# The third quarter of the first weights, loaded behind batch 0's gathers, and a new order of all steps

## The chip, the cores and the metric

The kernel runs on one core of a Trainium2 chip. Five engines work side by side and each takes its own queue strictly in program order: PE (TensorE, matrix products; PEld is its weight load), DVE (VectorE), ACT (ScalarE), POOL (GpSimd) and SP (SyncE, which here only issues DMAs). The metric is the time of one execution on the device in microseconds (us).

## The reference

Eight batches of eight heads, 576 positions, 64 values per head. Attention is masked (four heads see the last 32 positions, four see every 32nd), its output is laid side by side to rows of 512, a two-dimensional Fourier transform is added, and each row goes through a normalised two-layer network.

```python
def _attn_ref(q, k, v):
    scores = scale * np.matmul(q, k.transpose(0, 1, 3, 2))
    ...
    scores = np.where(masks[None, :, :, :], scores, -1000000000.0)
    ...
    return np.matmul(attn, v).astype(np.float32)

def _moe_ref(x, w_ch1, w_ch2):
    X = np.fft.fft(x, axis=1)
    X = np.fft.fft(X, axis=2)
    mixed = np.real(X).astype(np.float32)
    u = x + mixed
    mu = np.mean(u, axis=-1, keepdims=True)
    var = np.mean((u - mu) ** 2, axis=-1, keepdims=True)
    un = (u - mu) / np.sqrt(var + 1e-06)
    ch = np.maximum(un @ w_ch1, 0.0) @ w_ch2
    return (u + ch).astype(np.float32)
```

Here w_ch1 is 512 x 2048 and w_ch2 is 2048 x 512. Both arrive as 64-bit floats.

## The kernel before

**Stages.** Each batch goes through attention for four pairs of heads (`att_first` for batch 0, `att_pair32` and `att_pair` for the others), whose outputs `xo` are written to a buffer `xd` in DRAM. From there `fft_load` reads the first half of the rows in order (`xa`, line 820, on SP) and the mirrored rows by four gathers on POOL (line 824, into the third part of `xa` and the three of `xb`). `fft_batch` folds the rows on DVE and POOL (E and O are sum and difference of `xa` and `xb`, then `tmp` and `FD`, all line 834), and two products follow: A (lines 977 and 978 for batch 0, 931 and 932 later) against tables of cosines and sines and B (1003; 954 later). Their sum with x is `u`, the input of the network. `u` is cut into 18 chunks of 256 rows. Each chunk is normalised, transposed by DMA (`uT`, line 1084), multiplied with the first weights in eight steps (`ups`, line 1278, into `ph`) and with the second weights in eight (`downs`, line 1317, into `acc`). These two lines hold most of PE's work, and all products are made with 16-bit halves, three products for one.

**The weights.** Each of the two weight matrices comes in 16 pieces of 128 x 512, 64 bits an element. `weights` loads one into a staging buffer (line 1104 where there is a fixed place, 1108 from a pool) and turns the 64-bit patterns into 32-bit floats by hand: two passes on ACT (1113 and 1117; the second also on DVE, 1119), one on DVE (1123), then the sign, another on DVE (1129) or on ACT and POOL. `gram_piece` multiplies each piece with itself on PE (1158). After each four pieces of the first weights, `quarter` takes the norms from that product (1176 to 1178, a small product at line 332, `scales`), and `split` makes the two 16-bit halves with the scale so found (1197 on ACT, 1199 on DVE). `weights2` does the same for all 16 pieces of the second weights at once, and `scaled` splits them (1232, 1234), with a DMA (1236) to put one half in its place. The first `downs` needs these. While a gram is open, `rest` fills PE's planned pauses with products of a zero matrix (line 1166), whose results change nothing.

**Where the third quarter stands.** Pieces 0 to 7 of the first weights are loaded into the place of their own later results. Pieces 8 to 11 are loaded into the tiles that held q and k of batch 0 (`q0s`, by `stg1`), so a load has to wait until that head's scores are made. Pieces 12 to 15 are taken into buffers of later phases, behind the event `xb0`, which batch 0's gathers set.

**What sets the order.** There is no hand-written order. Every step is a generator that yields an `Op` with an engine, a planned duration, buffers that it takes (`get`) and returns (`put`), events it needs and sets. `Order.run` is a small simulator inside the kernel's construction: it takes the step that can start first on its engine, and among those that can start within a small window (the `W..` numbers) the one of lowest bias. What it picks is emitted to the engine's queue, so the plan fixes the order of every queue, and the chip then runs each queue in order as semaphores allow. The biases, windows, lead times and penalties are the numbers of `P`: for example `c` for the tables of batch 0 (`consts`), `w0a` for pieces 0 to 11, `w0` for 12 to 15, `GL` the time allowed to land for the gathers of batches 1 to 7, `GL0` for batch 0's. `vo` says behind which head's q and k the value tables are loaded, and `S0` and `S1` in which staging buffers pieces 12 to 15 and those of the second weights land.

The plan is made in two parts. In the first part are `att_first`, pieces 0 to 11 with quarters 0 to 2, `consts`, and `fft_batch(0)` up to product A, which needs the event `second`. It is run until nothing more can go; then the buffers of the start are given up and `second` is set. So in every queue all steps of the first part come before all of the second. In `consts` and for pieces 12 to 15 a helper `late` ties the first DMA that is issued after the gathers to the last gather, by a real wait; all behind it on SP's queue wait with it.

Of the kernel before, what the change touches and what calls it, by code (L numbers as in the profile page):

```python
# [19 lines left out]
B, H, S, D = 8, 8, 576, 64  # L20

P = dict(
    SL2=1.57, SLD2=2.778, GL0=8, LAT=0.637, GL=6.45, t2=9.759, l0=-28.888, a0=-20, sq0=7.465, w0a=25.925, c=-26.309,
    z=12.736, f0=-22.976, w0=-25.887, s0=-1.061, w1=2.262, s1=-12.582, p0=-14.949, p1=10.996, pn=-3.093, a1=-18.418,
    f1=-1.718, a2=1.463, f2=8.266, an=8.66, fn=-33.229, db=1.762, up=20.1, dn=20.114, ev=0.829, WS=0.0, WV=0.068,
    WA=0.0, WG=0.789, WT=0.095, SL=0.0, SLD=1.95, np=3, AL=3.136, SG=2.918, Lcl=0.553, Lfs=-0.174, Lwl=4.986,
    Lul=-7.793, LO=-11.521, LE=4.84, Lc2=-1.49, LSD=-13.798, Lsub=2.836, Lsub0=20.543, Lrt=20.361, Lu=4.381,
    ORD0=(3, 2, 0, 1), vo=([], [], [], [0, 1, 2, 3]), S0=('qk', 'qk', 'kt', 'pt'),
    S1=('kt', 'pt', 'f6', 'u', 'uT', 'qk', 'f6', 'kt', 'uT', 'u', 'f6', 'kt', 'pt', 'uT', 'u', 'f6'), HB=4, RB=1,
)  # L30
ORD0 = P["ORD0"]
FP32 = {(b, hp) for b in range(3) for hp in range(4)}
# [121 lines left out]
AL, SG = P["AL"], P["SG"]  # L154
# [19 lines left out]
WT = {e: P["W" + e] for e in "SVAGT"}  # L174
# [95 lines left out]
op = Op  # L270
# [3 lines left out]
def body(ctx: ExitStack, tc: tile.TileContext, a, out):  # L274
# [14 lines left out]
    SL, SLD = P["SL"], P["SLD"]  # L289
# [88 lines left out]
    def att_pair(b, hp):  # L378
# [20 lines left out]
        A.activation(jk[0:vp, 0:vw], vn[0:vp, 0:vw], AF.Square, accum_out=ss[0:vp, 2:3])  # L399
        yield op("T", 0.06, get="big", note=f"total {nm}", slack=P["SL2"])  # L400
        pn = psbig(f"n{nm}")[:, 0:3]
# [43 lines left out]

        yield op("T", 0.75 if local else 0.6, get="big", put="kt", note=f"scores {nm}", slack=P["SL2"])
        ps = psbig(f"s{nm}")
# [172 lines left out]
    def att_first(sp, pw):  # L620
# [11 lines left out]
        G.memset(pbt, 0.0)  # L632
        f6s = {hp: f6(f"pt0_{hp}") for hp in ORD0}
        for hp in ORD0:
# [195 lines left out]
    def fft_batch(b, xab=None):  # L830
# [85 lines left out]
        for gs in ((0, 1), (2,), (3, 4)):  # L916
            first, last = gs[0] == 0, gs[-1] == 4
            endT = yield op("T", 0.5 * len(gs), get="big f6 -fft" if first else "acc" if one and len(gs) == 1 else "big", need=f"FH{257 if last else 0}_{b} csin second", put="f6" if last else "", note=f"A{gs[0]} {b}", slack=P["SL2"] if b > 2 else SL if b else 0)
            if first:
# [28 lines left out]
        for t in range(3):  # L948
            r = 128 if t < 2 else 33
            yield op("T", 0.68, get=("acc" if one else "big") + (" u" if t < 2 else ""), need=" ".join(f"AT{g}_{b}" for g in (0, 2, 3)) + " dftd", put="f6" if t == 2 else "", at=endT, note=f"B{t} {b}", slack=P["SL2"] if b > 2 else SL if b else 0)  # L950
            ps = psone(b, f"B{b}_{t}")[:, 0:512]
# [144 lines left out]
    def weights(wi, i):  # L1096


        src, W, _ = list(wpieces(wi))[i]
        kind = STG[wi][i]  # L1100
        if kind is None:
            yield op("S", 1.45, need=f"sc{ORD0[(i - 8) // 2]}" if i >= 8 else "", note=f"ld {wi} {i}")
            stg = stg1(i)
            nc.sync.dma_start(stg, src)
        else:
            yield op("S", 1.45, get=kind, need="xb0", note=f"ld {wi} {i}")
            stg = stg2(kind, f"sa{wi}_{i}")
            late(nc.sync.dma_start(stg, src))
        wds = stg.bitcast(I32).rearrange("p (n t) -> p n t", t=2)
        wl, wh = wds[:, :, 0], wds[:, :, 1]  # L1110
        yield op("A", 0.67, note=f"c1 {wi} {i}")

        A.activation(wh.bitcast(F32), wh.bitcast(F32), AF.Copy, scale=2.0**-112)
        o = op("A", 0.67, note=f"cl {wi} {i}", alt=dict(V=(0.47, P["Lcl"])))
        yield o
        if o.engine == "A":
            A.activation(wl, wl.bitcast(U32), AF.Copy, scale=2.0**-29 * (1 - 2.0**-10), bias=-0.499)
        else:
            V.tensor_scalar(wl, wl, 29, None, op0=ALU.logical_shift_right)
        yield op("V", 0.8, need=f"w0_{i}" if wi else "", note=f"c2 {wi} {i}")  # L1120
        F = W.rearrange("p a b -> p (a b)").bitcast(F32)
        Fi = F.bitcast(I32)
        V.scalar_tensor_tensor(out=Fi, in0=wh, scalar=3, in1=wl, op0=ALU.logical_shift_left, op1=ALU.bitwise_or)  # L1123
        spawn(gram_piece(wi, i, F))

        o = op("V", 0.8, note=f"c3 {wi} {i}", alt=dict(A=(0.67, SG)))
        yield o
        if o.engine == "V":
            V.scalar_tensor_tensor(out=Fi, in0=wh, scalar=-(2**31), in1=Fi, op0=ALU.bitwise_and, op1=ALU.bitwise_or)  # L1129
        else:  # L1130
            A.activation(wl.bitcast(F32), wh.bitcast(F32), AF.Sign)
            yield op("G", 1.4, note=f"c4 {wi} {i}")
            G.tensor_tensor(out=F, in0=F, in1=wl.bitcast(F32), op=ALU.mult)
        yield op(o.engine.replace("A", "G"), 0, put=kind or "", sets=f"sign{wi}_{i}", note=f"c5 {wi} {i}")
# [314 lines left out]
```

## Time and profile before

| | |
|---|---|
| time, median of 3 runs | 983.55 us (978.34 to 986.63) |
| the profiled execution: time | 983.61 us |
| its span, first to last instruction | 981.8 us |
| PE busy | 939.3 us, 96% |
| DVE busy | 574.7 us, 59% |
| ACT busy | 452.2 us, 46% |
| POOL busy | 286.3 us, 29% |
| fill products (line 1166), all before 120 us | 427, 34.0 us of PE's busy time |
| granted PE clock, mean | 0.973 |

Busy time counts the fill products and the half-speed stretches too, so 96% isn't all useful work. A span of 40 equal slices is 24.5 us each in the page; the row of the granted clock there is 7, 8, 6, 8, 9, 9, 8 tenths in the first seven and 9 in all later ones. Nearly all that isn't steady lies in the first 200 us. In the rows below, "idle before" in brackets is the time that the engine waited ahead of the instruction, and behind the arrow stands what ended that wait by the profile; x is a count of instructions merged into one row, and a row can have short pauses in it.

### The profile page before, as it was taken

To read this page: it belongs to the slowest core of one execution; us is meant where nothing else is said; L and a number is where in the kernel's file an instruction comes from. 1 tells how busy PE (TensorE), PEld (TensorE's weight loads), DVE (VectorE), ACT (ScalarE), POOL (GpSimd) and SP (SyncE) were. 2 spreads that over 40 slices of the span, in tenths; PEclk is the share of its full clock that TensorE was granted. 3 is DMA by queue.
4 is the path that set the end of the run, shared out by engine and by line. 5 is a ranking of instruction groups with operands and counts; after the bars stand their busy time and mean duration, and the time that the engine had idled before them with its cause. 6 is when DMAs were issued, how large, how long until landed. Compare 5 with 4: busy or idle time off the path is not lost.

```text
span 981.8 us, 23873 instructions
## 1 busy us (share of the span) xinstructions
PE 939.3 (96%) x10017; PEld 659.7 (67%) x10018; DVE 574.7 (59%) x1129; ACT 452.2 (46%) x891; POOL 286.3 (29%) x297
## 2 busy tenths in 40 slices
PE   6779879999999999999999999999999999999998
PEld 6657764676766667676766676667666676676674
DVE  5785896756888588758765957587727221202000
ACT  2744765354565366555745564556423322222121
POOL 0120221223433343334324422442334122222121
PEclk7868998999999999999999999999999999999999
DMA  9757536804533644184537442743240101201000
GB/s 296 240 196 262 170 109 213 187 17 134 133 104 83 150 154 113 35 173 136 123 70 191 97 113 39 225 96 97 59 120 11 34 18 33 32 12 43 1 23 21
DMA packets 135452, 107.12 MB, mean 109 GB/s; under 512 B 103337, under 2 KB 113833, under 8 KB 135345
## 3 DMA queue, kind: packets, MB, share of 16 engines
q1 hardware_dynamic: 132784, 97.22, 37.0%
q0 software_dynamic: 2560, 8.39, 2.8%
q8 instruction: 78, 1.28, 0.6%
q14 instruction: 30, 0.24, 0.1%
HBM read 64.24 MB, written 18.89 MB: 85 GB/s over the span
## 4 chain that ended last, share of the span: by engine, by line
PE 82%; DVE 8%; DMA 5%; ACT 2%; issue 1%; SPq 1%; POOL 0%; ACTq 0%; DVEq 0%; POOLq 0%
PE ph L1278 35%; PE acc L1317 35%; PE B L954 2%; DMA uT<-unp 2%; PE A L931 1%; PE s L456 1%; DMA W<-in_w 1%; DVE W L1123 1%; PE o L487 1%; PE A L978 1%; PE A L977 1%; DMA mloc<-in_mloc 1%; DVE W L1129 1%; PE o L494 1%; DMA q<-in_w 1%
## 5 line engine op out<-in xcount | busy, mean ns | idle before, releaser
L1278 PE MATMUL ph<-uT,W 128*128 128x256 f16 x3456 | 395.4, 273 | 3.3 <-DMA uT<-unp 2.1
L1317 PE MATMUL acc<-W,h 128*128 128x512 f16 x1728 | 390.1, 381 | 2.1 <-POOL ss L393 1.6
L1278 PEld LDWEIGHTS <-W 128*128 128x128 f16 x3456 | 335.2, 98 | 53.8 <-DMA uT<-unp 2.4
L1296 POOL TENSOR_TENSOR h<-hf,h 128x512 f16<-128x512 f32 x144 | 184.5, 1282 | 461.2 <-ACT h L1294 337.8
L1317 PEld LDWEIGHTS <-h 128*128 128x128 f16 x1728 | 166.5, 98 | 191.7 <-issue 5.8
L1293 ACT ACTIVATE hf<-ph 128x512 f32<-128x512 f32 x144 | 85.8, 596 | 299.3 <-PE ph L1278 268.1
L1294 ACT ACTIVATE h<-ph 128x512 f16<-128x512 f32 x144 | 85.3, 592 | 0.0
L1325 DVE SCALAR_TENSOR_TENSOR u<-acc,cout,u 128x512 f32<-128x512 f32 x32 | 23.3, 745 | 101.5 <-PE acc L1317 100.4
L1082 DVE TENSOR_TENSOR unp<-un,unp 128x512 f16<-128x512 f32 x36 | 33.5, 932 | 48.3 <-ACT unp L1079 48.2
L1073 DVE TENSOR_SCALAR un<-u,mv,rstd 128x512 f32<-128x512 f32 x32 | 19.1, 596 | 52.1 <-POOL rstd L1066 50.8
L1066 POOL TENSOR_TENSOR rstd<-mv,negh 128x1 f32<-128x1 f32 x36 | 23.5, 657 | 76.1 <-DVE mv L1063 75.9
L433 DVE SCALAR_TENSOR_TENSOR kt<-qk,sc,kt 128x576 f16<-128x576 f32 (+1 forms) x40 | 36.6, 954 | 12.0 <-ACT kt L418 9.0
L1045 ACT ACTIVATE pq<-B,fcm 128x128 f32<-128x128 f32 (+7 forms) x105 | 27.3, 377 | 16.0 <-PE B L954 8.2
L1166 PE MATMUL gram<-oneb,zero 128*128 128x128 bf16 x427 | 34.0, 246 | 0.0
L468 ACT ACTIVATE sm<-sm 128x594 f32<-128x594 f32 (+1 forms) x20 | 16.3, 816 | 34.8 <-DVE sm L751 34.7
L1166 PEld LDWEIGHTS <-zero 128*128 128x128 bf16 x427 | 30.9, 113 | 2.0 <-issue 1.2
L418 ACT ACTIVATE kt<-qk,sc 128x576 f16<-128x576 f32 (+1 forms) x40 | 29.4, 788 | 3.9 <-DVE sc L374 3.2
L1079 ACT CAST unp<-un 128x512 f16<-128x512 f32 x36 | 22.1, 615 | 16.9 <-DMA uT<-unp 8.8
L1037 DVE TENSOR_TENSOR rt<-pq 128x257 f32<-128x257 f32 (+1 forms) x42 | 17.1, 449 | 21.7 <-ACT pq L1045 19.4
L751 DVE TENSOR_TENSOR sm<-sm,mx 128x594 f32<-128x594 f32 (+1 forms) x32 | 29.4, 919 | 0.3
L749 DVE TENSOR_REDUCE mx<-sm 128x11 f32<-128x594 f32 (+1 forms) x32 | 29.0, 907 | 0.4
L944 DVE SCALAR_TENSOR_TENSOR AT<-A,AT 128x290 f16<-128x290 f32 (+3 forms) x35 | 15.4, 481 | 21.5 <-ACT AT L939 20.5
(202 smaller groups left out, 1044.8 us busy)
## 6 DMA issues: line engine op xcount, KB each, us to landing
qk<-in_qk SPq DMA_DIRECT2D x28, 592.0 KB
sa<-in_w SPq DMA_DIRECT2D x20, 512.0 KB
out<-u SPq DMA_DIRECT2D x32, 256.0 KB
vn<-in_vl SPq DMA_DIRECT2D x10, 432.0 KB
W<-in_w SPq DMA_DIRECT2D x8, 512.0 KB
xd<-xo SPq DMA_DIRECT2D x16, 256.0 KB
xa<-xd SPq DMA_DIRECT2D x8, 512.0 KB
vn<-in_vs SPq DMA_DIRECT2D x10, 384.0 KB
```

Of the source, the lines that this page charges most:

```text
L418: A.activation(hi, src, AF.Copy, scale=f)
L433: V.scalar_tensor_tensor(out=lo, in0=src, scalar=f, in1=hi, op0=ALU.mult, op1=ALU.subtract)
L749: V.tensor_reduce(out=mx[:, 0:nb], in_=sm, axis=AX.X, op=ALU.max)
L751: on(o).tensor_tensor(out=sm, in0=sm, in1=mx[:, 0:nb].rearrange("p (g o) -> p g o", o=1).to_broadcast([128, nb, w]), op=ALU.subtract)
L1045: A.activation(dst, ps[0:r, c0:c1], AF.Copy, scale=cm[0:r])
L1082: on(o).tensor_tensor(out=unp[:, 1], in0=un, in1=unp[:, 0], op=ALU.subtract)
L1166: T.matmul(idle[-1][:, 0:128], zerb, oneb, start=False, stop=False)
L1278: T.matmul(ph[:, i, :], W1[:, 4 * (f0 // 512) + d, x, f0 % 512 : f0 % 512 + 128], self.uhl[y][:, d, :], start=(n == 0), stop=(n == 11))
L1293: A.activation(hf, ph, AF.Relu, scale=HS)
L1294: A.activation(hh, ph, AF.Relu, scale=HS)
L1296: G.tensor_tensor(out=hl, in0=hf, in1=hh, op=ALU.subtract)
L1317: T.matmul(self.acc[s], (hh, hl)[x][:, i, 128 * s : 128 * s + 128], W2[:, f, 1 - y, :], start=(f == 0 and n == 0), stop=(f == 15 and n == 2))
```

## The change

One line of `weights` changes: what the loads of pieces 8 to 11 need in the plan. Before it was the event that the scores of the head are made whose tile the piece takes; now it is `xb0`, that batch 0's gathers have landed. The staging place stays the same. Beside it, most of the numbers of `P` change, and with them the order of all queues; among them `vo`, so that the value tables of batch 0 are loaded between the heads' q and k instead of behind all of them, and `S1`, the staging places of the second weights.

```diff
 P = dict(
-    SL2=1.57, SLD2=2.778, GL0=8, LAT=0.637, GL=6.45, t2=9.759, l0=-28.888, a0=-20, sq0=7.465, w0a=25.925, c=-26.309,
-    z=12.736, f0=-22.976, w0=-25.887, s0=-1.061, w1=2.262, s1=-12.582, p0=-14.949, p1=10.996, pn=-3.093, a1=-18.418,
-    f1=-1.718, a2=1.463, f2=8.266, an=8.66, fn=-33.229, db=1.762, up=20.1, dn=20.114, ev=0.829, WS=0.0, WV=0.068,
-    WA=0.0, WG=0.789, WT=0.095, SL=0.0, SLD=1.95, np=3, AL=3.136, SG=2.918, Lcl=0.553, Lfs=-0.174, Lwl=4.986,
-    Lul=-7.793, LO=-11.521, LE=4.84, Lc2=-1.49, LSD=-13.798, Lsub=2.836, Lsub0=20.543, Lrt=20.361, Lu=4.381,
-    ORD0=(3, 2, 0, 1), vo=([], [], [], [0, 1, 2, 3]), S0=('qk', 'qk', 'kt', 'pt'),
-    S1=('kt', 'pt', 'f6', 'u', 'uT', 'qk', 'f6', 'kt', 'uT', 'u', 'f6', 'kt', 'pt', 'uT', 'u', 'f6'), HB=4, RB=1,
+    SL2=0.915, SLD2=2.5, GL0=8, LAT=0.97, GL=20.106, t2=9.759, l0=-30.073, a0=-19.177, sq0=7.465, w0a=20.686,
+    c=-24.962, z=2.714, f0=-26.63, w0=-28.483, s0=0.533, w1=1.247, s1=-14.997, p0=-16.817, p1=10.038, pn=-3.534,
+    a1=-17.166, f1=-1.58, a2=10.531, f2=1.591, an=11.643, fn=-36.503, db=1.762, up=20.1, dn=20.117, ev=0.829, WS=0.0,
+    WV=0.071, WA=0.0, WG=0.677, WT=0.154, SL=0.0, SLD=1.664, np=3, AL=3.818, SG=2.188, Lcl=2.011, Lfs=-0.174,
+    Lwl=4.927, Lul=-1.506, LO=-10.812, LE=4.723, Lc2=-1.124, LSD=-15.782, Lsub=8.559, Lsub0=20.543, Lrt=20.361,
+    Lu=4.381, ORD0=(3, 2, 0, 1), vo=([], [0], [1, 2], [3]), S0=('qk', 'qk', 'kt', 'pt'),
+    S1=('u', 'pt', 'f6', 'kt', 'qk', 'uT', 'f6', 'kt', 'uT', 'u', 'f6', 'kt', 'pt', 'uT', 'u', 'f6'), HB=4, RB=1,
 )
 ...
         if kind is None:
-            yield op("S", 1.45, need=f"sc{ORD0[(i - 8) // 2]}" if i >= 8 else "", note=f"ld {wi} {i}")
+            yield op("S", 1.45, need="xb0" if i >= 8 else "", note=f"ld {wi} {i}")
             stg = stg1(i)
             nc.sync.dma_start(stg, src)
```

Nothing is computed otherwise: the same products, the same loads, in another order.

## The prediction

> **What bounds the kernel now.** I read the page's head first, then a table of busy time by stage, then the queues around the moved loads one by one.
>
> ```profile
> span 981.8 us, 23873 instructions
> PE 939.3 (96%) x10017; PEld 659.7 (67%) x10018; DVE 574.7 (59%) x1129; ACT 452.2 (46%) x891; POOL 286.3 (29%) x297
> ```
>
> ```profile
> 40.00:64.80 24.80, 15.54 (x196) 13.69 (x194) 22.89 (x40) 10.35 (x20) 9.37 (x9) 0.81 0.83 313
> 64.80:79.80 15.00, 14.66 (x42) 8.47 (x43) 5.67 (x13) 7.33 (x13) 1.09 (x1) 0.50 0.31 107
> 79.80:107.40 27.60, 23.29 (x347) 19.92 (x348) 23.30 (x53) 18.27 (x33) 1.13 (x2) 0.95 0.83 266
> 107.40:148.90 41.50, 31.62 (x437) 27.61 (x435) 34.38 (x67) 25.60 (x44) 14.18 (x9) 0.98 0.42 128
> ...
> 200.00:981.80 781.80, 775.16 (x8001) 533.49 (x7999) 425.23 (x840) 349.13 (x710) 246.31 (x260) 1.00 0.34 84
> ```
>
> In the second fence the columns are stage and length, then busy time of PE, PEld, DVE, ACT and POOL, then the granted clock, the DMA share and GB/s. From 200 us to the end PE is busy 775.16 of 781.8 us at clock 1.00. No reordering can shorten that stretch by more than its 6.6 us of idle time, and the matmuls in it are the same before and after. So the change can only earn or cost time in the first 200 us, and only if it moves the point from which PE always has real work. Three stretches there are loose. PE is idle for 9.3 us in 40 to 64.8; it works at half clock (0.50) through the 15 us of batch 0's first FFT product A; and it is idle for 9.9 us between the first up-projection (107.4) and the first down-projection (148.9). DVE carries the first stretch: 22.89 of 24.80 us.
>
> The loads that the change moves stand here, on SyncE's queue, and the gathers beside them on GpSimd:
>
> ```profile
> 36.22 1.15 SPq L776 DMA_DIRECT2D xd<-xo  x2
> 37.48 1.86 SPq L1104 DMA_DIRECT2D q<-in_w  x3
> 41.87 0.38 SPq L820 DMA_DIRECT2D xa<-xd  x1
> 42.30 0.46 SPq L1104 DMA_DIRECT2D q<-in_w  x1
> 51.35 0.33 SPq L362 DMA_DIRECT2D f32a<-in_f32a  x1
> ...
> 53.21 2.05 SPq L1108 DMA_DIRECT2D sa<-in_w  x4
> ```
>
> ```profile
> 43.13 1.19 POOL L824 DMA_INDIRECT xa<-xd,ridx  x1 [40.34 <-DMA q<-in_w]
> ...
> 47.29 1.20 POOL L824 DMA_INDIRECT xb<-xd,ridx  x1 [0.30 <-issue]
> ```
>
> Three pieces of the third quarter are issued (37.48) between the last write of batch 0's attention (36.22) and its read back (41.87), and the fourth (42.30) just ahead of the gathers. f32a, which has to wait for the first of the gathers' landings that is still open, goes out at 51.35, so the gathers land near 51.3. The profile even names the piece loads as what released the first gather.
>
> What A waits for is on PE's own queue:
>
> ```profile
> 49.66 4.85 PE L1166 MATMUL gram<-oneb,zero 128*128 128x128 bf16 x84
> 58.07 0.41 PE L1158 MATMUL gram<-W 128*128 128x128 bf16 x4 [3.56 <-DVE W L1123]
> ...
> 64.66 0.16 PE L332 MATMUL gram<-s1w,oneb 128*128 128x1 bf16 x1 [0.72 <-DVE s1w L1178]
> 64.76 0.72 PE L977 MATMUL A<-f32a,E 128*65 128x145 f32 x2
> ```
>
> A starts at 64.76, 0.10 us after the small product that sums the third quarter's norms (64.66). This isn't a coincidence of data. The program is planned in two parts, and A needs the event "second", which is set only once the first part is all laid out. Quarters 0 to 2 of the first weights belong to the first part. So on PE the grams of pieces 8 to 11 and this norm product precede A in the instruction stream, before and after the change. This is the fact on which I set the forecast: whatever delays the third quarter delays A.
>
> **The change part by part.**
>
> *1. The moved loads.* Four DMAs leave their places at 37.48 and 42.30 and go behind the event that the gathers set. That frees 1.86 and 0.46 us of SyncE's issue, and 2.1 MB (4 x 128 x 512 x 8 bytes) leave the DMA engines while the write, the read back and the gathers run. What the write costs without them is shown by the head before it:
>
> ```profile
> 32.07 1.78 DMA xd<-xo
> ```
>
> That write took 1.78 us to land. The last one ended its issue at 37.37 and the read back that needs it went out at 41.87, 4.5 us. If it lands in 1.78 us, the gathers start 2.7 us sooner. The bounds are 0 (the two small-packet writes differ and the load has no share) and 4.5 us. I take 2.7, since that row is the same instruction in the same 6 us. The gathers land near 48.6 then; the four gather issues (43.13 to 48.49) are GpSimd's own and don't shrink.
>
> *2. What the loads meet behind the gathers.* There, by the planner's rules, f32a and f32b go first (the lower bias), then pieces 8 to 10, csin, and piece 11, because csin's thread waits for the tables to land in the plan and the pieces' threads don't. By shapes: 0.445 + 0.541 + 0.445 + 2.10 = 3.53 MB. The stage row gives 313 GB/s at a share of 0.83, so 377 GB/s for full engines, and 3.53 MB take 9.4 us. With a first landing of 1.8 us as above, piece 11 is in SBUF at 48.6 + 9.4 + 1.8 = 59.8. Then its path to A: two passes on ACT, one on DVE, four grams and the norm.
>
> ```profile
> L1113 ACT ACTIVATE q<-q 128x512 f32<-128x512 f32 x4 | 2.7, 672 | 2.1 <-DMA q<-in_w 2.1
> L1123 DVE SCALAR_TENSOR_TENSOR W<-q 128x512 int32<-128x512 int32 x4 | 2.6, 683 | 0.0
> L1117 ACT ACTIVATE q<-q 128x512 int32<-128x512 uint32 x4 | 2.6, 668 | 0.0
> L1129 DVE SCALAR_TENSOR_TENSOR W<-q,W 128x512 int32<-128x512 int32 x4 | 3.5, 885 | 0.0
> L1199 DVE SCALAR_TENSOR_TENSOR W<-W,scl,W 128x512 f16<-128x512 f32 x16 | 11.0, 747 | 1.4 <-ACT W L1197 1.4
> ```
>
> ```profile
> 63.81 0.28 DVE L1176 TENSOR_TENSOR gd<-gram,ident 128x128 f32<-128x128 f32 x1
> ```
>
> That is 0.67 + 0.67 + 0.68 + 0.41 = 2.4 us, and from the norm's first step (63.81) to A (64.76) 0.95 us: A at 59.8 + 3.4 = 63.2 by the transfers.
>
> *3. The same by DVE.* In the stretch DVE does batch 0's folds and the weights in turn:
>
> ```profile
> 53.12 1.75 DVE L834 TENSOR_TENSOR E<-xa,xb 128x1536 f32<-128x1536 f32 x1
> ...
> 57.33 0.69 DVE L1123 SCALAR_TENSOR_TENSOR W<-q 128x512 int32<-128x512 int32 x1
> ...
> 58.51 1.38 DVE L1129 SCALAR_TENSOR_TENSOR W<-q,W 128x512 int32<-128x512 int32 x1
> ...
> 60.35 0.68 DVE L1123 SCALAR_TENSOR_TENSOR W<-q 128x512 int32<-128x512 int32 x1
> ...
> 62.47 1.43 DVE L834 TENSOR_TENSOR FD<-E 128x381 f32<-128x381 f32 x2
> ```
>
> From 53.12 to the end of the last fold at 63.90 are 10.8 us. In them lie two of the four L1123 and one L1129 of the third quarter (two L1129 ended as E began, one follows A's start). After the change all four L1123 and, at least, three L1129 fall behind the gathers: 2 x 0.68 + 2 x 0.885 = 3.1 us more. E can begin at 48.6 and not at 53.12 (4.5 sooner: 2.7 from the gathers, 1.8 because the weights that ran until 53.12 are gone). So the folds end at 48.6 + 10.8 + 3.1 = 62.5, and with the norm's 0.95 A comes at 63.5. Transfers say 63.2 and DVE 63.5, against 64.76: a gain of 1.3 us. The ends are a gain of 5 (only the folds count, if the plan puts the weights into waits of the chain) and a loss of 4 (the gathers land at 51.3 as before and DVE, in order, stands before piece 11: 51.3 + 9.4 + 1.8 + 3.4 = 65.9, and up to 2.9 us of folds behind it).
>
> *4. The fourth quarter.* Its loads (53.21, x4) go behind the third's: 2.1 MB / 377 GB/s = 5.6 us later. Their cover is the stage from 64.8 to 79.8, where DMA has a share of 0.31, DVE is busy 5.67 and ACT 7.33 of 15 us: nothing. If that cover goes (A sooner than its weights), their DVE work meets the stage to 107.4, where DVE has 4.3 us free.
>
> *5. The first loads (vo).* Values now go between the heads' q and k; the last head's q and k come behind three value tables, about 1.25 MB by shape, 4.0 us at 313 GB/s.
>
> ```profile
> 14.44 1.54 PE L702 MATMUL pT<-ident,pbd 128*128 128x128 f32 x6
> ...
> 19.86 1.05 DVE L751 TENSOR_TENSOR sm<-sm,mx 128x864 f32<-128x864 f32 x1
> ...
> 27.09 0.92 ACT L688 ACTIVATE sm<-sm 128x864 f32<-128x864 f32 x1
> ```
>
> The last head's subtraction ends at 20.91 and its exponential starts at 27.09, behind weight passes on ACT: 6.2 us cover the 4.0. On the other side the first head's transposes (14.44) may no longer stand behind the last head's scores. I take 0: the last head decides when the gathers start, and it keeps its place behind ACT. Ends: 3 us gained, 4 lost.
>
> *6. All the other numbers.* Penalties, lead times and staging buffers change, so every queue after 60 us is ordered anew. No row shows the new order. From 200 on it can earn 6.6 us at most; in 107.4 to 148.9 it can earn up to 9.9. It can lose as much by a new gap of that size. I take 0, in the middle.
>
> The sum: this execution took 983.61 us around a span of 981.8 (the median of the runs is 983.55, so the two stand together). 983.6 - 1.3 = 982.3, with everything behind A moved by that much: 982.
>
> **A rule against the change.** Behind 84 fill products PE idles 3.56 us before the gram at 58.07, and the clock is 0.50 throughout A. The Trainium skill, "TensorE: Matmul & The Clock Gate", Part 1, says that an idle window of about 3.4 us puts the array to half rate, and that as long a busy one releases it; this trace agrees with the first half, with 3.56 us and 0.50.
>
> **The rivals.**
>
> *The clock (0.10).* The grams that now break up 45 to 61 us come later, so PE rests longer ahead of A and B may also run at half clock. Half clock costs a factor of 1.8 on the same eight transposes:
>
> ```profile
> 23.64 1.94 PE L702 MATMUL pT<-ident,sm 128*96 128x128 f32 x8 [0.72 <-ACT sm L688]
> ...
> 28.06 1.08 PE L702 MATMUL pT<-ident,sm 128*96 128x128 f32 x8 [0.24 <-ACT sm L688]
> ```
>
> ```profile
> 82.88 0.11 PE B L999
> ...
> 89.47 0.12 PE B L1004
> ```
>
> The first two thirds of B, which u needs, run from 82.88 to 89.59; 0.8 x 6.7 = 5.4 us more, with the 1.3 of the main case 988. Against it: PE ran at half clock through all of A and was released before B, without a pause.
>
> *Faster (0.30): the new order closes the wait for the second weights.* If the second weights' conversion ends sooner, half of the 9.9 us between 107.4 and 148.9 goes; and if A gets fill up to its start and so the full clock, 15 us become 15 / 1.8 = 8.3, 6.7 less. Both: 983.6 - 5 - 6.7 = 972; with A 3 us sooner, 969. For it: DVE and ACT are half idle in A's stage. Against it: nothing in the moved loads reaches there by itself.
>
> *Slower (0.15): the third quarter pushes the second weights.* Its twelve DVE operations on four pieces (0.68 + 0.885 + 0.75 each, 9.3 us) run after 64.8 rather than before, and the second weights' staging buffers come free that much later. Then the first down-projection starts at 158 and not at 148.9; PE, with the up-projection done, idles, and restarts at half clock once more:
>
> ```profile
> 148.92 5.28 PE acc L1317 x12
> ...
> 155.22 2.59 PE acc L1317 x12
> ```
>
> Twelve products cost 5.28 us after the pause and 2.59 later, 2.7 more; such a restart is in this run already, so it is counted half. 983.6 + 9.3 + 1.3 = 994. It decides once A's stage can't take that work, when less than its free DVE time of 9.3 us is left.
>
> **How the numbers follow.** Main case 0.45, at 982, by its own bounds of 5 gained and 4 lost 978 to 987. Changes under 1% (9.8 us) can't be told from none here, so faster means below 973.7 and slower above 993.4. Faster: 0.30, and 0.02 of the main case by part 6. Same: 0.41 of the main case and 0.09 of the clock's. Slower: 0.15, 0.02 of the main case and 0.01 of the clock's. The range from 968 to 993 leaves out the outer parts of the two far cases, near 0.2.
>
> **What would show it.** Right: piece loads of the third quarter issued behind f32a; gathers starting near 40.4; E near 48.6; A still directly behind the norm product of the third quarter, at 63 to 64; the down-projection starting within 2 us of 148.9. Part 1 is wrong if the gathers start at 43 all the same. Part 2 is wrong if A starts well ahead of 62 or behind 67. The forecast as a whole is wrong if idle and fill time ahead of 200 us, which are what can change, move by 10 us: that would be the new order's doing, which I set at 0.

## The result and the profile after

| | before | after |
|---|---|---|
| median of 11 runs each | 979.49 us (975.78 to 986.63) | 991.0 us (987.59 to 995.79) |
| the profiled execution, time and span | 983.61 and 981.8 us | 991.29 and 989.5 us |
| granted PE clock in it | 0.973 | 0.972 |

The ratio is 1.0104, with a 95% interval from 1.0074 to 1.0134. The change makes the kernel slower by about 1%. The time lies inside the range that was given, but the likeliest case (982 us, no change that can be told) didn't come: a gain of 1.3 us was forecast and a loss came.

The head of the page after, with the group of the fill products (busy us and mean ns of one, then the idle time before):

```profile
span 989.5 us, 24054 instructions
PE 944.7 (95%) x10121; PEld 667.1 (67%) x10122; DVE 586.3 (59%) x1129; ACT 452.0 (46%) x891; POOL 282.1 (29%) x297
L1166 PE MATMUL gram<-oneb,zero 128*128 128x128 bf16 x531 | 40.5, 242 | 0.2 <-issue 0.2
```

PE is busy 5.4 us longer than before, but 6.5 us of that are fill (40.5 against 34.0). The real work is the same to 1.1 us. So the 7.7 us by which the span grew are time in which PE had nothing real to do. The busy time by stage, in the same stretches as before (PE, PEld, DVE, ACT, POOL, then clock, DMA share, GB/s):

```profile
64.80:79.80 15.00, 14.10 (x63) 9.39 (x64) 8.13 (x19) 7.34 (x13) 0.00 (x0) 0.61 0.79 298
79.80:107.40 27.60, 22.99 (x283) 20.16 (x283) 17.89 (x41) 19.38 (x35) 0.00 (x0) 0.75 0.64 212
107.40:148.90 41.50, 36.34 (x489) 31.34 (x491) 36.76 (x77) 19.91 (x35) 8.88 (x9) 1.00 0.36 104
```

From 107.4 to 148.9 PE is idle for 5.2 us and not for 9.9, but 6.73 us of its busy time there are fill now and 0.18 were before: without fill it has no real work for 11.9 us, before for 10.1. From 79.8 to 107.4 the clock fell from 0.95 to 0.75 and DVE's busy time from 23.30 to 17.89 us: there something waits.

Fixed stretches cut through work that has moved. The better cut is by events: the start of batch 0's product A, the first up-projection, and two fixed points behind. The two views below give it for before (first fence) and after (second): stretch and length, PE's busy time, clock, DMA share, GB/s.

```profile
0.00:64.76 64.76, 45.57 (x724) 0.82 0.81 269
64.76:107.40 42.64, 37.99 (x388) 0.79 0.65 210
107.40:160.00 52.60, 42.69 (x551) 0.94 0.47 147
160.00:280.00 120.00, 116.06 (x1238) 0.99 0.49 125
280.00:981.80 701.80, 696.99 (x7125) 1.00 0.33 83
```

```profile
0.00:68.80 68.80, 46.96 (x764) 0.83 0.77 254
68.80:124.50 55.70, 45.96 (x481) 0.81 0.62 204
124.50:160.00 35.50, 34.34 (x428) 1.00 0.45 115
160.00:280.00 120.00, 111.95 (x1309) 0.96 0.51 139
280.00:989.50 709.50, 705.50 (x7154) 1.00 0.32 81
```

The fill products among these are, in the same view of line 1166 alone, 25.47 us (then 8.37, 0.18, 0, 0) before and 27.07 (then 13.47, 0, 0, 0) after. Length less busy time plus fill is the time that PE spends on nothing. "Lost" is used for it from here on:

| PE's lost time, us | up to A | A to first up-projection | from there to 160 | 160 to 280 | 280 to the end | sum |
|---|---|---|---|---|---|---|
| before | 44.7 | 13.0 | 10.1 | 3.9 | 4.8 | 76.5 |
| after | 48.9 | 23.2 | 1.2 | 8.0 | 4.0 | 85.3 |
| difference | +4.2 | +10.2 | -8.9 | +4.1 | -0.8 | +8.8 |

With 1.1 us less of real work these are the 7.7 us of the span. The difference of the medians is larger (11.5 us) because the profiled execution of before was itself one of the longer ones, 4.1 us above its later median. Now the rows behind the columns, in the order of time.

*Up to A.* SyncE's and GpSimd's queues after:

```profile
34.29 1.19 SPq L776 DMA_DIRECT2D xd<-xo  x2
40.30 0.38 SPq L820 DMA_DIRECT2D xa<-xd  x1
51.48 0.35 SPq L362 DMA_DIRECT2D f32a<-in_f32a  x1
52.40 1.34 SPq L1104 DMA_DIRECT2D q<-in_w  x3
```

```profile
41.53 1.13 POOL L824 DMA_INDIRECT xa<-xd,ridx  x1 [38.74 <-ACT W L1197]
```

The loads do stand behind f32a now. But from the last write of `xd` (its issue ends at 35.48) to the read that needs it (40.30) are 4.8 us, with no load issued between; before it was 4.5 with three. The DMA engines weren't empty here (three other pieces were issued just ahead of that write, and the DMA share is 1.01 and 0.96 from 34 to 38 us), so the plainer comparison is e1 below, the kernel before with the one line changed: 4.4 us. And from the first gather to f32a, which waits for the gathers, are 10.0 us (9.0 in e1) where it was 8.2. The gathers land no sooner: f32a goes out at 51.48, before at 51.35. What the profile names as the first gather's releaser was a piece load before and is a split on ACT now, but in both kernels the gather starts 1.2 to 1.3 us behind the read of `xa`.

DVE's queue shows what A then waits for:

```profile
48.84 2.74 DVE L1199 SCALAR_TENSOR_TENSOR W<-W,scl,W 128x512 f16<-128x512 f32 x4 [0.79 <-ACT W L1197]
51.68 1.76 DVE L834 TENSOR_TENSOR E<-xa,xb 128x1536 f32<-128x1536 f32 x1
...
59.68 2.37 DVE L1123 SCALAR_TENSOR_TENSOR W<-q 128x512 int32<-128x512 int32 x2
...
66.28 0.69 DVE L1129 SCALAR_TENSOR_TENSOR W<-q,W 128x512 int32<-128x512 int32 x1
```

DVE's folds run from 51.68 to 59.76 in one piece, and all eight conversions of the third quarter (lines 1123 and 1129) follow them, up to 66.97. Before, seven of the eight stood between the folds or ahead of them. So A comes 17.1 us behind the start of E, where it was 11.6.

*From A to the first up-projection.* PE and DVE after:

```profile
68.69 0.18 PE L332 MATMUL gram<-s1w,oneb 128*128 128x1 bf16 x1
68.80 0.72 PE L977 MATMUL A<-f32a,E 128*65 128x145 f32 x2
...
86.20 1.56 PE L1003 MATMUL B<-f32b,AT 65*128 65x65 f32 x10
...
97.08 1.82 PE L515 MATMUL s<-qk 64*64 64x96 f32 x36 [2.50 <-DMA qk<-in_qk]
...
99.02 2.72 PE L1003 MATMUL B<-f32b,AT 65*128 65x65 f32 x10
```

```profile
104.94 0.75 DVE L1008 TENSOR_TENSOR u<-B,xa 128x257 f32<-128x257 f32 x2 [5.81 <-PE B L1004]
...
112.93 1.28 DVE L1129 SCALAR_TENSOR_TENSOR W<-sa,W 128x512 int32<-128x512 int32 x2
114.14 0.69 DVE L1060 BATCH_NORM_STATS2 st<-u 128x6 f32<-128x512 f32 x1
```

and the same two steps of DVE before:

```profile
89.62 0.76 DVE L1008 TENSOR_TENSOR u<-B,xa 128x257 f32<-128x257 f32 x2 [1.34 <-PE B L1004]
90.29 0.68 DVE L1060 BATCH_NORM_STATS2 st<-u 128x6 f32<-128x512 f32 x1
```

A follows the third quarter's norm product by 0.11 us, as before, only 4.0 us later. Then comes what is new. In PE's new order the scores of batch 1's third pair of heads (line 515, 36 products) stand between B's first block of columns (84.6 to 87.7) and its second (from 99.0); before, all of B came first. Their q and k, loaded at 89.00, land at 96.94, and PE waits 2.50 us with B's second block queued behind. After that wait it runs at half clock: ten products take 2.72 us and not 1.56. DVE has nothing to do for 5.81 us and gets the sum `u` at 104.94, 15.3 us later than before. Then its own new order puts conversions of the second weights ahead of the first chunk's statistics: 114.14 is 9.2 us behind `u`, and not 0.67. The first up-projection starts at 124.5 and not at 107.4.

*From there on* the plan repays most of that: the second weights are further on when the up-projections start, so PE waits 1.2 us up to 160 and not 10.1. But near 240 a new pause stands, between batch 0's chunks and batch 1's (PE after):

```profile
240.11 0.18 PE L332 MATMUL n<-ss,oneb 128*128 128x3 bf16 x1 [1.68 <-DVE vsum L562]
...
244.81 0.26 PE L456 MATMUL s<-kt 64*64 64x54 f16 x4 [4.53 <-ACT kt L418]
```

### The profile page after: what moved, and what is told of

Read it like the earlier page. It is cut to its first block, busy times and chain, and to the rows that moved or that the text cites. A ratio compares the mean times of both kernels' runs of the same rounds, so it can differ in the third digit from the quotient of the medians.

```text
span 989.5 us, 24054 instructions
## 1 busy us (share of the span) xinstructions
PE 944.7 (95%) x10121; PEld 667.1 (67%) x10122; DVE 586.3 (59%) x1129; ACT 452.0 (46%) x891; POOL 282.1 (29%) x297
## 4 chain that ended last, share of the span: by engine, by line
PE 86%; DVE 5%; DMA 4%; SPq 1%; issue 1%; ACT 1%; POOL 0%; DVEq 0%; ACTq 0%; POOLq 0%
PE ph L1278 38%; PE acc L1317 36%; PE B L954 2%; PE s L456 2%; PE A L931 1%; DMA q<-in_qk 1%; PE B L1003 1%; PE o L487 1%; DMA uT<-unp 1%; DMA W<-fs 1%; DMA qk<-in_qk 1%; DMA W<-in_w 1%; PE o L494 1%; PE A L977 1%; PE A L978 1%
## 5 line engine op out<-in xcount | busy, mean ns | idle before, releaser
L1278 PEld LDWEIGHTS <-W 128*128 128x128 f16 x3456 | 335.4, 98 | 51.3 <-issue 1.0
L1296 POOL TENSOR_TENSOR h<-hf,h 128x512 f16<-128x512 f32 x144 | 181.4, 1260 | 484.7 <-ACT h L1294 344.0
L1073 DVE TENSOR_SCALAR un<-u,mv,rstd 128x512 f32<-128x512 f32 x32 | 21.3, 666 | 79.2 <-POOL rstd L1066 78.4
L1166 PE MATMUL gram<-oneb,zero 128*128 128x128 bf16 x531 | 40.5, 242 | 0.2 <-issue 0.2
L1166 PEld LDWEIGHTS <-zero 128*128 128x128 bf16 x531 | 37.2, 110 | 3.2 <-issue 2.9
L1158 PE MATMUL gram<-W 128*128 128x128 bf16 x128 | 14.1, 247 | 17.5 <-DVE W L1123 16.2
L824 POOL DMA_INDIRECT xa<-xd,ridx x8 | 12.4, 1544 | 61.4 <-ACT W L1197 38.7
L944 DVE SCALAR_TENSOR_TENSOR AT<-A,AT 128x290 f16<-128x290 f32 (+3 forms) x35 | 15.1, 480 | 22.3 <-ACT AT L939 22.2
```

The lines of the kernel that those rows point to most:

```text
L1166: T.matmul(idle[-1][:, 0:128], zerb, oneb, start=False, stop=False)
L1278: T.matmul(ph[:, i, :], W1[:, 4 * (f0 // 512) + d, x, f0 % 512 : f0 % 512 + 128], self.uhl[y][:, d, :], start=(n == 0), stop=(n == 11))
L1296: G.tensor_tensor(out=hl, in0=hf, in1=hh, op=ALU.subtract)
```

## The experiments

Three theories were set against each other. *Gate*: A comes later because it stands behind the third quarter, whose loads now go behind the gathers, and that is the loss. *Order*: the new numbers order PE and DVE worse between A and the first up-projection, and that is the loss. *Valley*: PE runs dry near 240 because batch 1 is late, whatever happens ahead of it. Ratios are to the kernel before on the same chip, with 95% intervals. All lost times are worked out as above. E, A and the first up-projection ("first up") are starts, in us, in the one profiled execution of each run.

| run | median us | ratio | E at | A at | first up at | lost, 160 to 280 |
|---|---|---|---|---|---|---|
| e1 need only | 1002.47 | 1.024 [1.0176, 1.0304] | 52.0 | 69.1 | 122.2 | 13.6 |
| e2 numbers only | 983.36 | 1.0054 [1.0017, 1.0091] | 52.0 | 63.6 | 113.5 | 6.6 |
| e3 old vo | 988.56 | 1.0105 [1.0058, 1.0152] | 50.2 | 67.4 | 123.3 | 8.1 |
| e5 one number back | 997.6 | 1.0229 [1.0149, 1.031] | 50.2 | 67.3 | 115.0 | 20.9 |
| e6 half the loads moved | 1008.86 | 1.027 [1.0239, 1.0301] | 50.3 | 64.4 | 115.4 | 20.0 |
| e7 third quarter in the second part | 1019.0 | 1.0387 [1.0352, 1.0422] | 52.0 | 59.8 | 118.9 | 8.4 |
| e8 the same in the kernel before | 989.91 | 1.0112 [1.0067, 1.0156] | 50.2 | 60.3 | 112.0 | 5.0 |
| e9 batch 1 not waiting | 1004.61 | 1.0242 [1.0204, 1.0279] | 52.3 | 69.4 | 125.7 | 10.0 |
| e10 loads ahead, same order | 993.22 | 1.0127 [1.0077, 1.0176] | 49.3 | 66.4 | 127.1 | 8.9 |
| e12 B first, same order | 991.34 | 1.0116 [1.0073, 1.0159] | 53.2 | 70.3 | 125.6 | 8.5 |
| e13 both | 987.97 | 1.008 [1.0029, 1.0131] | 50.6 | 67.7 | 121.7 | 8.1 |
| e14 the changed kernel again | 994.35 | 1.016 [1.0122, 1.0198] | 53.4 | 70.5 | 122.4 | 8.2 |

**The two halves of the change.** e1 is the kernel before with the new line of `weights` alone; e2 is the changed kernel with the old line.

```diff
# e1, against before
-            yield op("S", 1.45, need=f"sc{ORD0[(i - 8) // 2]}" if i >= 8 else "", note=f"ld {wi} {i}")
+            yield op("S", 1.45, need="xb0" if i >= 8 else "", note=f"ld {wi} {i}")
# e2, against after
-            yield op("S", 1.45, need="xb0" if i >= 8 else "", note=f"ld {wi} {i}")
+            yield op("S", 1.45, need=f"sc{ORD0[(i - 8) // 2]}" if i >= 8 else "", note=f"ld {wi} {i}")
```

> The kernel before with only the one line of the loads changed (pieces 8 to 11 need the gathers), all numbers as before. Theory 'load': A stands behind the third quarter on PE, so A starts at 68 to 69 us as in the changed kernel, not at 64.8, and the time is 5 to 8 us above before (985 to 988 against 979.5). Theory 'order' (the changed kernel loses because batch 0's product B is cut in two by the scores of batch 1): here B stays in one piece, so A is late all the same, but the time stays within 3 us of before.

> The changed kernel with the loads of pieces 8 to 11 put back ahead of the gathers, all new numbers kept; in its plan B is in one piece. Theory 'load': A starts near 64.8 us again and the whole loss is gone, 978 to 982. Theory 'order': the same 978 to 982 here, because B is whole; the two part in the other kernels. A third theory, that the new numbers cost time later (a stall near 240 us), gives 985 or more.

Measured: before 978.73 in that job; the line alone +2.4%, the numbers alone +0.5%, both +1.0% (in another job). So the line with the old numbers costs 23.7 us, far more than A's delay of 4 us can be, and with the new numbers some 7 (11.5 less e2's 4.6; some 10 by e14, which stands 15.1 above before). The line doesn't only move four loads: it changes the plan's times, and with them every queue behind. In both kernels B is one block again (in e1 from 82.6 to 99.2, mostly at half clock), so what B's parting costs isn't seen here. In e2 the lost time between A and the first up-projection is 18.1 us (before 13.0, after 23.2): half of what the change loses there comes with the numbers alone.

The table's E and A show what the line does to A. In every run with the new line and the quarter in the first part, A starts 17.1 us behind E; in e2 and before, 11.6 us. The order on DVE sets that, folds first and conversions behind; e10 below tells it from the landing of the loads.

**The value tables.** e3 takes back the old places of their loads.

```diff
-    Lu=4.381, ORD0=(3, 2, 0, 1), vo=([], [0], [1, 2], [3]), S0=('qk', 'qk', 'kt', 'pt'),
+    Lu=4.381, ORD0=(3, 2, 0, 1), vo=([], [], [], [0, 1, 2, 3]), S0=('qk', 'qk', 'kt', 'pt'),
```

> The changed kernel with the value tables loaded behind all heads' q and k again; order from A on is the same as in the changed kernel. Theory 'load' and theory 'order' both expect no difference beyond 2 us, since the last head's path has slack behind ACT (989 to 993). If the value tables matter, the first head's output comes 4 us sooner, the gathers land sooner than 51.4 us and the time falls by up to 4 us.

The ratio is that of the change itself (1.0105 against 1.0104). `vo` is worth nothing that can be measured here; the interval is half a per cent, or 5 us, to each side.

**One number of the order.** With `w1`, the lead of the second weights, back at its old value, the rest as after, B comes as one block ahead of the scores.

```diff
-    c=-24.962, z=2.714, f0=-26.63, w0=-28.483, s0=0.533, w1=1.247, s1=-14.997, p0=-16.817, p1=10.038, pn=-3.534,
+    c=-24.962, z=2.714, f0=-26.63, w0=-28.483, s0=0.533, w1=2.262, s1=-14.997, p0=-16.817, p1=10.038, pn=-3.534,
```

> The changed kernel with one number put back (w1, the bias of the second weights, 1.247 to 2.262), which puts B into one piece ahead of batch 1's scores; loads stay behind the gathers. Theory 'order': the first up-projection starts near 110 us rather than 124.5 and the time falls by 5 us or more, to 980 to 986. Theory 'load': A still starts near 68.9 us, and the time stays at 988 to 992.

The up-projection does start 9.5 us sooner than after (115.0), and still the kernel is slower: by 6.6 us if the medians of the two jobs are compared (997.6 against 991.0), by 1.2% if their ratios to before are. PE's timeline in e5 shows where it went:

```profile
240.25 0.26 PE L456 MATMUL s<-kt 64*64 64x54 f16 x4 [4.72 <-ACT kt L418]
247.05 0.18 PE L332 MATMUL n<-ss,oneb 128*128 128x3 bf16 x1 [4.76 <-ACT jk L399]
252.89 7.07 PE L1278 MATMUL ph<-uT,W 128*128 128x256 f16 x48 [5.65 <-DMA uT<-unp]
```

Three pauses of 4.7 to 5.7 us, where after has one of 4.53. An earlier start of the first up-projection that a new plan buys can be lost again 130 us on. The theory of the order, put as "the first up-projection alone sets the time", is refuted.

**Moving the gate.** e6 moves only pieces 10 and 11 behind the gathers. e7 takes the third quarter out of the first part of the plan, so that A doesn't stand behind it, and stages it in buffers of the network; e8 does the same to the kernel before.

```diff
# e6, against after
-            yield op("S", 1.45, need="xb0" if i >= 8 else "", note=f"ld {wi} {i}")
+            yield op("S", 1.45, need=("xb0" if i >= 10 else f"sc{ORD0[(i - 8) // 2]}") if i >= 8 else "", note=f"ld {wi} {i}")
# e7 against after, e8 against before
-    STG = [None] * 12 + list(P["S0"]), P["S1"]
+    STG = [None] * 8 + ["u", "u", "uT", "uT"] + list(P["S0"]), P["S1"]
...
-        for i in range(12):
+        for i in range(8):
...
-        for q in range(3):
+        for q in range(2):
...
-    for i in range(12, 16):
+    for i in range(8, 16):
...
+    spawn(quarter(2), bias=P["s0"] - 0.1)
```

> The changed kernel with only pieces 10 and 11 behind the gathers; 8 and 9 are loaded as before. Theory 'gate' (A stands behind the third quarter's grams on PE; the later the last of them lands, the later everything of batch 0 and, through the shared queues, batch 1): A starts about half way, at 65.5 to 67 us, and the time is between that of the kernel with all loads ahead (983) and the changed one (991), 984 to 990. Theory 'order' (the loss is in how the plan falls out and not in the loads): from A on PE's order is that of the kernel with w1 put back, so the time is that one's, 994 to 1000.

> The changed kernel with pieces 8 to 11 moved wholly into the second part of the plan (staged in tiles of u and uT), so that A no longer stands behind their grams on PE. Theory 'gate': A starts at 58 to 61 us, as soon as batch 0's folds are done, and the time falls below the changed kernel's, to 975 to 985. Theory 'order' or 'backlog' (the weights' work on DVE and ACT is the bound, wherever it stands): A is early, but batch 1 is no sooner, and the time stays at 985 or more.

> The kernel before with pieces 8 to 11 moved wholly into the second part of the plan, old numbers. Theory 'gate': A at 58 to 61 us and 970 to 982. Theory 'backlog': A early, time 980 to 1000, because the second weights and batch 1 wait for the same DVE and ACT work, now standing later.

A moves as the gate says: it starts 14.1 us behind E with half the loads (at 64.4, sooner than forecast), and at 59.8 and 60.3 without the gate. The time doesn't follow. All three are slower than the kernel that they were made from, e7 by 28 us. The first A in PE's timeline of e8, whose first up-projection stands at 111.96:

```profile
60.27 0.75 PE L977 MATMUL A<-f32a,E 128*65 128x145 f32 x2 [8.02 <-POOL E L834]
```

A is 4.5 us sooner than in the kernel before and the up-projection 4.5 us later. So A's start alone doesn't set the time either, and the gate by itself doesn't explain the loss.

**The wait for batch 1.** In e9 batch 1's transform reads the buffer of batch 0, so its gathers needn't wait for batch 1's attention. Batch 1's output isn't the reference's.

```diff
-        nc.sync.dma_start(xa[:, 0:2], xd[b][0 : 2 * HALF].rearrange("(t p) c -> p t c", t=2)[0:128])
+        nc.sync.dma_start(xa[:, 0:2], xd[0 if b == 1 else b][0 : 2 * HALF].rearrange("(t p) c -> p t c", t=2)[0:128])
...
-                out=dst, out_offset=None, in_=xd[b],
+                out=dst, out_offset=None, in_=xd[0 if b == 1 else b],
```

> The changed kernel, same order of all queues, but batch 1's transform reads batch 0's rows, so that it no longer waits for batch 1's attention (batch 1's output is therefore not the reference's). Theory 'valley' (the loss shows where PE runs out of work near 240 us, because batch 1's u comes late): batch 1's gathers start up to 14 us sooner, the pause near 240 us closes and the time falls by 4 to 9 us, to 981 to 986. Theory 'first rows' (the loss is the first up-projection at 124.5 instead of 107.4 us): nothing changes, 988 to 992.

The gathers of batch 1 start at 160.4 and not at 174.4, yet its first chunk is transposed at 239.5 (after: 237.0), and the pause near 240 stands. The theory of the valley, put as a wait for batch 1's attention, is refuted. What PE does up to there is other work that stands ahead in its queue. Why e9 is over 13 us slower than after isn't known; its profile shows half clock through all of A and B's first block (the second runs at full clock), and 8.6 us lost behind 280 rather than 4.0.

**The same order, two places changed.** The runs above all build a new plan. The last four, on one chip, keep the changed kernel's order on every queue but for the one or two places named. e10 issues the four loads by hand just ahead of the read of `xa`; e12 puts the scores of batch 1's third pair behind B's second block on PE; e13 does both; e14 is the changed kernel once more.

```diff
# e10
-        nc.sync.dma_start(xa[:, 0:2], xd[b][0 : 2 * HALF].rearrange("(t p) c -> p t c", t=2)[0:128])
+        [nc.sync.dma_start(stg1(i), list(wpieces(0))[i][0]) for i in range(8, 12) if b == 0]; nc.sync.dma_start(xa[:, 0:2], xd[b][0 : 2 * HALF].rearrange("(t p) c -> p t c", t=2)[0:128])
...
-            nc.sync.dma_start(stg, src)
+            if i < 8: nc.sync.dma_start(stg, src)
# e12
-        ps = psbig(f"s{nm}")
-        wk, off = scores32(ps, qk, local, n)
+        res = []; hold.append(lambda: (res.append(psbig(f"s{nm}")), res.append(scores32(res[0], qk, local, n)))); ((b, hp) == (1, 0)) or hold.pop()()
...
+        res or hold.pop()(); ps, (wk, off) = res
...
-            spawn(sums(b, t, r, xa, xb, ps[0:r, 0:257], ps[0:r, 512:769], "big"), bias=P["t2"] if t == 2 else None)
+            hold and hold.pop()(); spawn(sums(b, t, r, xa, xb, ps[0:r, 0:257], ps[0:r, 512:769], "big"), bias=P["t2"] if t == 2 else None)
```

> The changed kernel with its plan kept, so that every engine's order is the same; only the four loads of the third quarter are issued by hand on SyncE's queue just ahead of the read of xa, where the kernel before has them. Theory 'gate' (what the moved loads cost directly is that A stands behind the third quarter on PE): A starts at 63 to 65.5 us instead of 68.8 and the time falls by 3 to 8 us, to 983 to 988. Theory 'order' (the rebuilt order has taken the lateness up, the loss is elsewhere): A is early, but the time stays within 2 us of the changed kernel's.

> The changed kernel with its plan kept; only on PE the second block of batch 0's product B is issued ahead of the scores of batch 1's third pair of heads, which wait for their q and k. Theory 'cut' (the first up-projection is late because B is cut by those scores, and that costs the time): B's second block runs at 90 us instead of 99, the first up-projection starts 3 to 9 us sooner than 124.5 and the time falls by 3 to 8 us. Rival: DVE and the weights stand in front anyway, the first up-projection moves by less than 2 us and the time by less than 2 us.

> Both of the two edits before in one kernel: loads of the third quarter ahead of the read of xa, and B's second block ahead of the scores, all else in the changed kernel's order. If 'gate' and 'cut' are two causes in one chain, the gains add: the first up-projection at 112 to 117 us and 978 to 984 us. If either stands behind the other, the time is that of the better of the two alone.

> The changed kernel itself, as the measure for the three others on the same chip: 988 to 994 us, A at 68 to 70 us. If it lies above 1000, the chip or the run decides by more than the edits, and the slower reading of the kernel without batch 1's wait is explained by that.

Before took 979.25 in this job and the changed kernel 994.35. By the medians the loads ahead alone are worth 1.1 us, B first alone 3.0, both 6.4. The intervals of e10 and e12 overlap that of e14 widely, so the single gains aren't certain. That of e13 overlaps it by a little (1.0131 against 1.0122), but four of e13's five executions are faster than all five of e14's, so a gain of both together is likely, and its size is open. In e10 and e13 the loads are issued at 33 to 37 us, and still A comes 17.1 us behind E, as in e14: DVE's order is kept, with the conversions behind the folds. So in the changed order it isn't the landing of the loads that A waits for. In e13 A starts at 67.7 and B's second block is back at full clock ahead of the scores (PE, then DVE):

```profile
96.39 1.56 PE L1003 MATMUL B<-f32b,AT 65*128 65x65 f32 x10
...
99.61 1.04 PE L515 MATMUL s<-qk 64*64 64x96 f32 x36
```

```profile
100.94 0.74 DVE L1008 TENSOR_TENSOR u<-B,xa 128x257 f32<-128x257 f32 x2
...
110.87 0.68 DVE L1060 BATCH_NORM_STATS2 st<-u 128x6 f32<-128x512 f32 x1
```

DVE's wait of 5.81 us is gone. But the statistics still come 9.9 us behind `u`, behind the second weights' conversions, and the first up-projection starts at 121.7. Mending PE's order alone uncovers DVE's.

One more reading of these traces: the transposes of batch 1's first chunk start at 234.1 in e13, 235.0 in e14, 235.5 in e3, 237.0 after, 237.7 in e12 and 242.3 in e10, and from there to the end of the span all six take 752.0 to 752.8 us. So among these six every difference arises ahead of 242 us. (e9, in the same order, takes 761.0.) The kernel before starts them at 226.4 and takes 755.4 from there. The whole loss of the change, 10.6 us, stands ahead of that point, and 2.9 us come back behind it. No run was faster than the kernel before.

## Why the prediction was wrong

*Part 1, the moved loads: wrong.* The gathers were to start at 40.4 and land at 48.6. They start at 41.5 and land where they did, near 51.5. The step that failed is "if it lands in 1.78 us": that row is one link of the chain of waits, counted from the start of an issue, and not the time from the end of the write's issue to the read, which is 4.5 us with the loads beside it and 4.8 without (4.4 in e1). The loads held up neither the write nor the gathers. In e2, e10 and e13, where the loads are ahead, the first gather leads f32a by 8.6, 9.7 and 10.0 us; without them by 10.0 after, and by 9.0 in e1. For the landing of the gathers the lower bound of that part, 0, was the value.

*Parts 2 and 3, A behind the third quarter: the mechanism right, two terms of the sum mis-sized.* A stands directly behind the norm product in every run that keeps the quarter in the first part, at 66.4 to 70.5 in the changed order and 63.6 where the old line is back. Part 2's order of the loads came true, and ACT took piece 11 as it landed, at 63.08, where its sum gives 62.5 for gathers that land at 51.3. But forecast was 1.3 us gained by A, and measured are 4.0 lost. Part 3 had E at 48.6 and A at 63.5, 14.9 us behind. Measured are 51.68 and 17.1: 3.1 and 2.2 us more, the 5.3 by which A missed.

The first term is part 1's time carried on. E couldn't have begun at 48.6 in any case, since it stands behind the second quarter's splits in DVE's queue, which ran until 51.58. That "the weights that ran until 53.12 are gone" was a misreading: before, these splits (line 1199, 49.27 to 52.01) were among them, and they aren't the third quarter's. The second term is DVE's order. The forecast kept the conversions between the folds, with the folds ending last at 62.5; DVE's folds ended first, at 59.76, and all eight conversions, the norm and A came behind them. Loads that were in early (e10, e13) changed nothing of that. The measured 68.8 is the far end that part 3 gave for gathers at 51.3 (65.9 and 2.9 us of folds behind it), but what stood behind was conversions and not folds, so the agreement is luck.

*Part 4, the fourth quarter at nothing: not tried apart.* A's stage had room as read: DVE is busy 8.13 of 15 us there.

*Part 5, vo: nothing against it*, by e3, though its bounds of 3 us gained and 4 lost lie within that run's interval.

*Part 6, "I take 0, in the middle": a term put at nothing though no row showed it.* This step and part 3 share the lost direction. The new order loses 10.2 us between A and the first up-projection (5.1 of them with the numbers alone, by e2) and 4.1 near 240, and gains 8.9 between; with the tail and the real work it comes to 3.5 us lost. That adds up with part 3's miss of 5.5 us (4.2 lost, 1.3 forecast as gained): 982.3 + 5.5 + 3.5 = 991.3, the profiled time. This is the bookkeeping of one execution of each kernel, and the line and the numbers aren't parted in it. The bounds of 10 us each way held, but the middle between them was no estimate. The diff had a clue that I passed by: numbers retuned together with a line can be there to limit what the line costs. e1 shows that cost as 23.7 us with the old numbers.

*The rivals.* "Slower" had the direction: the second weights' conversions do meet the first chunk on DVE. The place was another one, ahead of the up-projection and not the first down-projection, which started at 153.9 against 148.9 and not at 158. "Faster" had one true half: PE's lost time from the first up-projection to 160 did shrink, from 10.1 to 1.2 us; nothing came of it, since more had been lost ahead of it. "The clock" was right that B would run at half clock, but it was another part of B, and behind another pause.

*What is shown and what stays open.* Shown: the loss arises ahead of batch 1's first chunk; neither A's start nor the first up-projection's sets the time by itself; A's delay comes from DVE's order; undoing the load's place and B's parting together in the same order gives 6.4, by the medians, of the 15.1 us that e14 stands above before. Open: which part of the new order costs the 8.7 us by which e13 is still above before. Two suspects are left on DVE: the 9.9 us between `u` and the statistics, and the 5.5 us more between E and A. Taking the conversions away from either place in the same order wasn't tried, nor were late loads in the order of before. What makes the pause near 240, if not the wait for batch 1's attention, is open too.

## What to carry to other kernels

Where a planner lays out all queues, a one-line change of what a step needs is a change of the whole order, and its price isn't the moved step's: here one line cost 2.4% and one number about 1%, while putting the moved loads back in the same order gave 1.1 us, which can't be told from nothing. Predict such a change by what each queue has ahead of the critical steps (here DVE ahead of E, and between E and A), give the new order a loss rather than zero where nothing shows a gain, and test it by edits that keep the order and move one thing. A gain at an early stage counts only if the stage that follows has nothing else in its queue.

## What the runs showed of the hardware

Executions of the same kernel differ by more than the change costs, and the granted clock goes with it. Before, nine executions of one job took from 973.84 us at a mean granted clock of 0.982 to 987.47 at 0.969: 13.6 us, where 0.013 of 980 us, an estimate of what the clock alone makes, is 12.7. In some executions product A ran at half clock throughout (e9 and e12), in others at full clock for a while, with the same queues up to there: from 70.0 to 73.2 us in the changed kernel's first profile, from 71.1 to 77.8 in e14. The Trainium skill, "TensorE: Matmul & The Clock Gate", Part 1, says that the ramp comes at a free-running window and differs from run to run, which fits, and puts its penalty under 1% of a typical span; here the spread of one kernel's executions is 1.4%, most of it the clock by the estimate above.

The Trainium skill, in the same section, puts an idle window of about 3.4 us ahead of half clock. In the changed kernel 2.50 us without a product, with 2.3 us of fill ahead of it, were followed by half clock; in e14 it was 2.01 us. That the pause was the cause isn't shown, since the clock fell to half in the middle of A too, with PE busy throughout. PE by stretches, after, in B (the last column but two is the clock):

```profile
94.60:97.00 2.40, 0.00 (x0) 1.00 1.04 239
97.00:99.00 2.00, 1.92 (x37) 0.54 0.99 309
99.00:104.70 5.70, 5.70 (x25) 0.50 0.43 145
```

and in A, with the busy time of all engines:

```profile
71.80:73.30 1.50, 1.50 (x9) 0.84 (x7) 1.50 (x3) 1.50 (x4) 0.00 (x0) 0.99 0.93 350
73.30:74.80 1.50, 1.50 (x5) 0.95 (x4) 0.13 (x1) 1.50 (x4) 0.00 (x0) 0.50 1.00 404
```

And 2.1 MB of loads ahead of the read and the four gathers, or beside them, didn't slow them. From the first gather to f32a it took 8.2 to 10.0 us with the loads (before, e2, e10, e13) and 9.0 to 10.3 without (after, e1, e3, e14); from the end of the write's issue to the read, 4.5 to 5.4 with and 4.4 to 5.0 without.
